# A gated-MLP kernel behind a dynamic convolution: another ramp, moved slots in eight superblocks, and a DMA that transposes for the last two

## The chip, the core and the metric

The kernel runs on one core of a Trainium2 chip. The core has TensorE (PE, matrix multiplies into PSUM), VectorE (DVE), ScalarE (ACT), GpSimd (POOL) and SyncE (SP), each with an instruction queue of its own that runs in order, and 16 DMA engines that work on the transfers which SyncE and GpSimd issue. The metric is the device time of the core in microseconds (us), the median of several executions. The profile is one further execution, recorded by the hardware profiler; its span is shorter than its device time by what lies around the program.

## What is computed

The input x has 8 sequences of 4096 tokens with 192 features. Each token has, for each of 8 heads of 24 features, 7 weights that go through a softmax. The convolution is causal: a token's output is the weighted sum of itself and the six tokens before it, with zeros ahead of a sequence's start. Then comes h = conv @ w_in (192 to 2048), g = h - tanh(h), and out = g @ w_out (2048 to 192).

```
w = exp(weight_gen - max);  w = w / (sum(w) + 1e-09)
x_pad = concatenate([zeros(B, 6, D), x], axis=1)
conv = einsum('bshk,bskhg->bshg', w, x_unf)      # k: 7 taps
h = conv @ w_in;  g = h - tanh(h);  out = g @ w_out
```

Inputs and outputs are float32; inside, the products, the convolution, g and both weight matrices are bfloat16.

## The kernel before

**Tiling.** The 32768 tokens are worked in 32 superblocks n of 1024 tokens. In SBUF a superblock lies with 8 consecutive tokens (j = 0 to 7) on each of 128 partitions. Its x tile (`x_t`, line 130) holds 14 rows of 192: the six tokens before (the halo) and the eight. Two such tiles exist and are used in turn. `load_wg` (L116) and `load_x` (L126) load with SyncE's DMAs.

**The convolution.** For a superblock the softmax is an exp on ScalarE (L169), sums and reciprocals on VectorE (L183, L198), and a scaling (L229) that writes the weights `wsm`. GpSimd multiplies x with the weights tap by tap (`products`, L299): taps 0 to 3 into `pa`, taps 4 to 6 into `pb`. VectorE takes a part of taps 0 and 1 off it (`help`, L250 and L251): it works on x of superblock n+2, and for superblocks 9 to 14 also on x of n+3, at f = 3 and f = 12 of the loop. The seven products are added in two places. DMAs issued by GpSimd that accumulate (`dma_sum`, L236) add `pb` onto `pa` and, from superblock 13 on, two taps of `pa` onto the other two (`second_sum`). What is left (two or four summands) is added by TensorE while it transposes: `conv_sums` (L384) multiplies with an identity and accumulates in PSUM, and ScalarE evicts the transposed convolution into `convT` (L410). There the 192 features lie as 3 slots c of 64 rows, and tokens are in columns; the lower 64 partitions hold even j, the upper 64 odd j, so that both halves of TensorE's rows work at once.

**The two matmuls.** The main loop runs over n and, inside, over 16 tiles f of 128 hidden features. `gemm1` (L427) does six matmuls on 64 rows, alternating between the halves, into one PSUM tile `ph` (three exist). ScalarE takes the tanh (L440), VectorE the difference `gt` (L441). The second matmul (L495) of superblock n-1 is cut into 128 pairs of matmuls on 64 rows, and a hand-written plan says how many pairs stand after each f (`pairs`), at which f and after how many pairs the transposes for superblock n+1 stand (`t1` for the third slot, `t2` for the first two), and at which f the softmax's two half sums stand (`sums`). Superblock 1 has the plan FIRST, 4 to 11 DOUBLE, the others STEADY. Results leave through ScalarE (L514) and SyncE's store (L518); the store of superblock n-2 stands at the start of superblock n.

**The ramp.** Superblocks 0 and 1 are prepared without the loop. There VectorE takes taps too, with weights that it reads from PSUM, and GpSimd reads weights from SBUF. So superblock 0 is scaled twice (once into SBUF, once into PSUM), and superblock 1 once into PSUM with a copy to SBUF by ScalarE (L221). The weight matrix w_in is loaded into the lower 64 partitions (`load_w_in`, L573), with feature 3u + c on partition u in slot c, and copied to the upper 64.

**Order.** Every engine runs its instructions in the order of the program text. A SyncE DMA that has to wait holds those behind it. SyncE's DMAs use eight completion counters in turn, and a DMA that reuses a counter waits until the one before on that counter has landed.

Of the kernel before, what the change touches and what calls it, by code (L numbers as in the profile page):

```python
# [16 lines left out]
def kernel(  # L17
# [28 lines left out]
    TWO_SUMS = (13, 14, 15, 16, 17, 18, 19, 20, 21, 22, 23, 24, 25, 26, 27, 28, 29, 30, 31)  # L46
    AHEAD = 4
# [3 lines left out]
    HELP = {n: ((n - 2, 3),) for n in (4, 5, 6, 7, 8, 9, 10, 11, 12, 13, 14, 15, 16, 17, 18, 19, 20, 21, 22, 23, 24, 25, 26, 27, 28, 29, 30, 31)} | {9: ((7, 3), (6, 12)), 10: ((8, 3), (7, 12)), 11: ((9, 3), (8, 12)), 12: ((10, 3), (9, 12)), 13: ((11, 3), (10, 12)), 14: ((12, 3), (11, 12))}  # L51
# [5 lines left out]
    RELIEF = ()  # L57
    assert S % TOK == 0 and D % R == 0 and F % P == 0
# [3 lines left out]
    xpool = ctx.enter_context(tc.tile_pool(name="xpool", bufs=2))  # L62
# [31 lines left out]
    conv_of = {}  # L94
    g_of = {}
# [19 lines left out]

    def load_wg(n):  # L116
        b, s = divmod(n, NSB)
        s0 = s * TOK
        wg_t = wgpool.tile([P, J, H, K], FP32, name="wg_t")
        nc.sync.dma_start(  # L120
            out=wg_t[:],
            in_=weight_gen[b, s0 : s0 + TOK].rearrange("(p j) h k -> p j h k", p=P),
        )
        wg_of[n] = wg_t

    def load_x(n, behind=None):  # L126
        b, s = divmod(n, NSB)
        s0 = s * TOK

        x_t = xpool.tile([P, HALO + J, D], FP32, name="x_t")  # L130

        def rows(p0, p1, r0=0, r1=HALO + J):
            first = x[0, 0:1]
            return nc.sync.dma_start(  # L134
                out=x_t[p0:p1, r0:r1, :],
                in_=bass.AP(
                    tensor=first.tensor,
                    offset=first.offset + (b * S + s0 + p0 * J - HALO + r0) * D,
                    ap=[[J * D, p1 - p0], [D, r1 - r0], [1, D]],
                ),  # L140
            )

        def no_halo():
            nc.sync.dma_start(  # L144
                out=x_t[0:1, 0:HALO, :],
                in_=zero[:].rearrange("o (h d) -> o h d", h=1).to_broadcast([1, HALO, D]),
            )


        if n == 0:  # L150
            rows(0, P, HALO, HALO + J)
            rows(16, P, 0, HALO)
            rows(1, 16, 0, HALO)
            no_halo()
        else:
            dma = rows(16 if s == 0 and ZERO_AT is None else 0, P)
            if behind is not None:
                order(dma, behind, "order of the loads")
            if s == 0 and ZERO_AT is None:
                rows(0, 16, HALO)  # L160
                rows(1, 16, 0, HALO)
                no_halo()
            elif s == 0:
                halo_of[n] = no_halo
        x_of[n] = x_t
# [40 lines left out]
    def softmax_norm_ramp(n, bank):  # L206
# [9 lines left out]
        wsm_v = bank[:, 0 : J * H * K].rearrange("p (j h k) -> p j h k", j=J, h=H)  # L216
        if n == 0 and SCALE_TWICE:
            scale(nc.vector, wsm[:], e_of[n], zr_v)
# [9 lines left out]
    def scale(eng, wsm, e_t, zr):  # L228
        return eng.tensor_mul(  # L229
            wsm.rearrange("p j h k -> p (j h) k"),  # L230
            e_t[:].rearrange("p j h k -> p (j h) k"),
            zr.rearrange("p (n o) -> p n o", o=1).to_broadcast([P, J * H, K]),
        )
# [9 lines left out]
    def help(n, ph, j):  # L243

        if n not in held:
            held[n] = (x_of[n], wsm_of[n][0], papool.tile([P, KA, J, D], BF16, name="pa"))
        x_t, wsm, pa = held[n]
        x_v = x_t[:]
        w = ph[:, 0, 0 : KH * H].rearrange("p (k h) -> p k h", k=KH)
        nc.vector.tensor_copy(w, wsm[:, j].rearrange("p h k -> p k h")[:, 0:KH])  # L250
        nc.vector.tensor_mul(  # L251
            pa[:, 0:KH, j, :].rearrange("p k (h g) -> p k h g", h=H),
            bass.AP(
                tensor=x_v.tensor,
                offset=x_v.offset + j * D,
                ap=[x_v.ap[0], [D, KH], [G, H], [1, G]],
            ),
            w.rearrange("p k (h o) -> p k h o", o=1).to_broadcast([P, KH, H, G]),
        )

    def products(n, taps=None, sums=None, hooks={}):
# [15 lines left out]
        x_v = x_t[:]  # L277
        step = x_v.ap[0]
# [6 lines left out]
        def mul(eng, k0, k1, j0=0, j1=J):  # L285

            if eng is nc.scalar:
                for j in range(j0, j1):
                    for h in range(H):
                        eng.activation(  # L290
                            out=prod(k0, k1)[:, 0, j, h * G : (h + 1) * G],
                            in_=x_t[:, k0 + j, h * G : (h + 1) * G],
                            func=ACT.Copy,
                            scale=wsm[:, j, h, k0 : k0 + 1],
                        )
                return
            w = wsm_v if eng is nc.vector else wsm[:]
            nj = j1 - j0
            return eng.tensor_mul(  # L299
                prod(k0, k1)[:, :, j0:j1].rearrange("p k j (h g) -> p k (j h) g", h=H),  # L300
                bass.AP(
                    tensor=x_v.tensor,
                    offset=x_v.offset + (k0 + j0) * D,
                    ap=[step, [D, k1 - k0], [G, nj * H], [1, G]],
                ),
                w[:, j0:j1]
                .rearrange("p j h (k o) -> p k (j h) o", o=1)[:, k0:k1]
                .to_broadcast([P, k1 - k0, nj * H, G]),
            )
# [15 lines left out]

        nt = len(HELP.get(n, ()))
        first = mul(nc.gpsimd, 0, KH, 0, J - nt)
        if n in PACED:

            order(first, pace_of[n - 3], "pace")  # L330
        if n in LAST_TAP:

            x_after[n + 1] = mul(nc.gpsimd, KH, KA - 1)
            second_sum(n - 1)
        else:
            mul(nc.gpsimd, KH, KA)
            second_sum(n - 1)
        if n not in LAST_TAP or n not in X_LATE:
            x_after[n + 1] = first

        def rest():
            if n in PART:
                dma_sum(pa[:, 0:2], pa[:, 2:4])
            mul(nc.gpsimd, KA, K)
            if n in PART:
                prods_of[n] = parts(4, 5, 6, 0, 1)
            else:
                dma_sum(pa[:, 0:3], pb[:, 0:3])
                if n in LAST_TAP:
                    mul(nc.gpsimd, KA - 1, KA)  # L350
# [5 lines left out]
                if n == NTOT - 1:  # L356
                    second_sum(n)

        return rest

    def second_sum(n):

        if n in to_sum:
            pa = to_sum.pop(n)
            dma_sum(pa[:, 0:2], pa[:, 2:4])

# [55 lines left out]
    def gemm1(n, f):  # L422
        convT = conv_of[n]
        ph = psum_h.tile([P, 2, HT], FP32, name="ph", tag="ph")
        for c in range(NC):
            for r in range(2):
                nc.tensor.matmul(  # L427
                    ph[:, r, :],
                    lhsT=w_in[r * R : (r + 1) * R, c, f * P : (f + 1) * P],
                    rhs=convT[r * R : (r + 1) * R, c, :],  # L430
                    start=(c == 0),
                    stop=(c == NC - 1),
                )
        th = tpool.tile([P, TOK], FP32, name="th")
# [73 lines left out]
    def store_out(blk):  # L508
# [6 lines left out]
        if j == J - 1:  # L515
# [3 lines left out]
                out=out[n * TOK : (n + 1) * TOK, :].rearrange("(p j) e -> p j e", p=P),  # L519
# [9 lines left out]
    def gemm2_last(j, f0=0, f1=NFT):  # L529
# [20 lines left out]
        ot = tpool.tile([P, D], FP32, name="ot", tag="th")  # L550
        nc.scalar.activation(out=ot[:], in_=po[:, 0, 0:D], func=ACT.Copy)
        nc.vector.tensor_add(out_sb[:, j, :], po[:, 1, 0:D], ot[:])
        if j % 2 == 1:
            nc.sync.dma_start(
                out=out[n * TOK : (n + 1) * TOK, :].rearrange("(p j) e -> p j e", p=P)[
                    :, j - 1 : j + 1, :
                ],
                in_=out_sb[:, j - 1 : j + 1, :],
            )

    w_in = const.tile([P, NC, F], BF16, name="w_in")
    w_out = const.tile([P, NFT, D], BF16, name="w_out")

# [28 lines left out]
    for c in range(NC):  # L592
        load_w_in(c, c + 1, 0, FA, last_exp[0] if c == 0 else None)
# [92 lines left out]
    DOUBLE = dict(pairs=(4, 12, 0, 16, 0, 16, 5, 11, 0, 5, 11, 6, 10, 0, 16, 16), t1=(15, 4), t2=(11, 4), scale=15, sums=(1, 10))  # L686
    DOUBLE_IN = (4, 5, 6, 7, 8, 9, 10, 11)

# [18 lines left out]
    for n in range(1, NTOT):  # L707
        more = n < NTOT - 1
        finish = []
        plan = FIRST if n == 1 else DOUBLE if n in DOUBLE_IN else APART if n in APART_IN else STEADY  # L710

        soft = [m for m in (n + 3 if n <= AHEAD else n + 4,) if m < NTOT]
        for f in range(NFT):
# [13 lines left out]
            elif f == 1:  # L727
                if soft:
                    softmax_exp(soft[0])
                if n + 2 < NTOT:  # L730
# [13 lines left out]
            for m in (n + 2, n + 3):  # L744
                if (n, f) in HELP.get(m, ()):
                    help(m, ph, J - 1 - HELP[m].index((n, f)))
            if n + 2 < NTOT and f == (9 if n == 1 else max([b for a, b in HELP.get(n + 2, ()) if a == n] + [3])):
# [4 lines left out]
            for chunks, at in sorted((((0, 1), plan["t2"]), ((2,), plan["t1"])), key=lambda c: c[1]):  # L752
                if more and at[0] == f:
# [3 lines left out]
                    if chunks == (2,):  # L757
                        finish = [softmax_norm(m, pc[:, 0]) for m in soft]
            if f >= plan["scale"]:
# [45 lines left out]
```

## Time and profile before

| | |
|---|---|
| median of 3 runs | 745.81 us (745.04 to 746.27) |
| the profiled execution: span | 743.4 us |
| TensorE busy | 722.3 us, 97% |
| VectorE busy | 687.4 us, 92% |
| GpSimd busy | 654.5 us, 88% |
| ScalarE busy | 638.8 us, 86% |
| first matmul L427 | 0.379 us mean, 3072 of them |
| second matmul L495 | 0.243 us mean, 7936 of them |
| granted TensorE clock | 0.995 of full speed, mean over the span |

Busy times of TensorE are made of overlapping records, so 97% doesn't say that it is at its peak. What the chain of waits says counts more: from 39 us on it is nearly all TensorE. A superblock takes 21.84 us at the end of the kernel and about 22.65 in superblocks 4 to 11, where the transposes add four summands instead of two. Superblock 31 ends with the second matmul alone, from 729.5 us.

The start of a superblock can be read from SyncE's stores, which stand some 3 us behind it. On the profile's clock superblock 7 begins near 176 us, superblock 8 near 198.7, superblock 30 at 684.3 and superblock 31 at 706.1.

### The profile page before, as it was taken

The page shows a single profiled execution, that of the slowest core. Times are in us where ns is not written, and L with a number is a line of the kernel's source. Part 1 is how long each engine was busy: PE and PEld are TensorE (multiplying, and loading weights), DVE is VectorE, ACT ScalarE, POOL GpSimd, SP SyncE. Part 2 cuts the span into 40 slices and gives each one's busy share as a digit, 9 for nine tenths or more (in the row PEclk, how much of TensorE's full clock was granted, in tenths as well). Part 3 has the DMA queues.
Part 4 walks back from the last instruction along what each step waited for, and adds up shares of the span by engine and source line. Part 5 has one row for each costly group of instructions (what it writes and reads, how often), then busy time and mean ns, then how long its engine had stood idle before and what let it go on. Part 6 is the DMA issues. An engine that isn't in the chain of part 4 may idle for free.

```text
span 743.4 us, 30037 instructions
## 1 busy us (share of the span) xinstructions
PE 722.3 (97%) x13616; PEld 556.5 (75%) x13616; DVE 687.4 (92%) x723; ACT 638.8 (86%) x872; POOL 654.5 (88%) x163
## 2 busy tenths in 40 slices
PE   3899999999999999999999999999999999999997
PEld 2477777778777777777777777777777777877777
DVE  7999899999999999999999999999999999988893
ACT  4888888888888888989889999898998989888882
POOL 7999999999999999999999999999999999991000
PEclk9899999999999999999999999999999999999999
DMA  8925367766567668878777977877887877776112
GB/s 236 245 46 161 135 172 185 195 179 149 124 183 184 183 185 224 210 199 203 166 202 209 236 186 204 178 195 205 221 209 195 192 181 194 193 149 110 45 45 86
DMA packets 34269, 130.06 MB, mean 175 GB/s; under 512 B 4591, under 2 KB 9439, under 8 KB 30174
## 3 DMA queue, kind: packets, MB, share of 16 engines
q0 software_dynamic: 19424, 51.12, 40.4%
q1 hardware_dynamic: 14718, 77.03, 27.6%
q8 instruction: 106, 1.74, 0.9%
q14 instruction: 21, 0.17, 0.1%
HBM read 54.52 MB, written 25.17 MB: 107 GB/s over the span
## 4 chain that ended last, share of the span: by engine, by line
PE 92%; DVE 5%; ACT 1%; issue 1%; DMA 1%; SPq 0%; DVEq 0%
PE ph L427 43%; PE obank L495 43%; PE pc L384 4%; DVE gt L441 3%; PE po L538 1%; ACT th L440 1%; DVE pa L299 1%; DMA wg_t<-in_weight_gen_dram 1%; DVE zsum L183 0%; SPq L134 0%; ACT convT L402 0%; DVE obank L211 0%; DVE pa L251 0%; DVE pb L299 0%; SPq L144 0%
## 5 line engine op out<-in xcount | busy, mean ns | idle before, releaser
L441 DVE TENSOR_TENSOR gt<-ph,th 128x1024 bf16<-128x1024 f32 x512 | 601.6, 1217 | 33.4 <-ACT th L440 23.2
L440 ACT ACTIVATE th<-ph 128x1024 f32<-128x1024 f32 x512 | 512.1, 1025 | 69.2 <-PE ph L427 60.3
L427 PE MATMUL ph<-convT,w_in 64*128 64x512 bf16 x3072 | 415.1, 379 | 5.3 <-DVE gt L441 3.3
L495 PEld LDWEIGHTS <-gt 64*128 64x128 bf16 x7936 | 355.6, 94 | 80.6 <-issue 6.3
L495 PE MATMUL obank<-w_out,gt 64*128 64x192 bf16 x7936 | 408.0, 243 | 0.9 <-issue 0.8
L299 POOL TENSOR_TENSOR pa<-x_t,wsm 128x2688 bf16<-128x2688 f32 (+3 forms) x68 | 338.9, 5232 | 0.2
L299 POOL TENSOR_TENSOR pb<-x_t,wsm 128x4608 bf16<-128x4608 f32 (+2 forms) x33 | 283.8, 8601 | 0.7 <-ACT wsm L221 0.5
L427 PEld LDWEIGHTS <-w_in 64*128 64x128 bf16 x3072 | 163.0, 94 | 86.0 <-issue 18.3
L514 ACT ACTIVATE out_sb<-obank 128x192 f32<-128x192 f32 x248 | 81.3, 328 | 11.2 <-PE obank L495 10.3
L410 ACT ACTIVATE convT<-pc 128x1024 bf16<-128x1024 f32 (+1 forms) x62 | 50.1, 810 | 2.9 <-PE pc L384 2.7
L236 POOL DMA_DIRECT2D pa<-pb x28 | 36.0, 1284 | 13.7 <-POOL pb L299 9.1
L384 PEld LDWEIGHTS <-pa 64*128 64x128 bf16 x2064 | 41.5, 100 | 6.8 <-DVE pa L299 1.1
L236 POOL DMA_DIRECT2D pa<-pa x21 | 34.7, 1651 | 9.6 <-DMA pa<-pb 8.9
L384 PE MATMUL pc<-ident,pa 64*128 64x64 bf16 x1968 | 41.2, 191 | 1.8 <-POOL pa L299 0.9
L183 DVE TENSOR_REDUCE zsum<-wg_t 128x32 f32<-128x224 f32 (+1 forms) x61 | 23.6, 387 | 2.9 <-ACT wg_t L169 2.9
L169 ACT ACTIVATE wg_t<-wg_t 128x448 f32<-128x448 f32 x32 | 18.2, 570 | 6.3 <-DMA wg_t<-in_weight_gen_dram 6.2
L251 DVE TENSOR_TENSOR pa<-x_t,ph 128x384 bf16<-128x384 f32 x34 | 18.8, 554 | 2.0 <-DVE ph L250 0.3
L229 DVE TENSOR_TENSOR wsm<-wg_t,pc 128x448 f32<-128x448 f32 x27 | 16.8, 621 | 2.5
L198 DVE RECIPROCAL pc<-zsum 128x64 f32<-128x64 f32 x27 | 14.9, 550 | 0.0
L384 PE MATMUL pc<-ident,pb 64*128 64x64 bf16 x216 | 4.9, 206 | 9.0 <-POOL pb L299 9.0
L384 PEld LDWEIGHTS <-pb 64*128 64x128 bf16 x288 | 6.3, 106 | 9.5 <-POOL pb L299 9.0
L538 PE MATMUL po<-w_out,gt 64*128 64x192 bf16 x256 | 11.2, 243 | 0.0
(27 smaller groups left out, 56.8 us busy)
## 6 DMA issues: line engine op xcount, KB each, us to landing
x_t<-in_x_dram SPq DMA_DIRECT2D x31, 1344.0 KB, 7.9
pa<-pb POOLq DMA_DIRECT2D x28, 1152.0 KB, 9.5
out_dram<-out_sb SPq DMA_DIRECT2D x31, 768.0 KB, 3.9
pa<-pa POOLq DMA_DIRECT2D x21, 768.0 KB, 7.2
wg_t<-in_weight_gen_dram SPq DMA_DIRECT2D x32, 224.0 KB, 7.1
x_t<-in_x_dram SPq DMA_DIRECT2D x1, 768.0 KB
w_out<-in_moe_w_out_dram POOLq DMA_DIRECT2D x1, 768.0 KB, 9.5
out_dram<-out_sb SPq DMA_DIRECT2D x4, 192.0 KB, 3.0
```

Source lines behind the costliest of these rows:

```text
L183: nc.vector.reduce_sum(out=zsum_of[n][:, j0 * H : j1 * H], in_=e_of[n][:, j0:j1].rearrange("p j h k -> p (j h) k"), axis=AX.X,)
L236: return nc.gpsimd.dma_start(out=out.rearrange("p k j d -> p k (j d)"), in_=in_.rearrange("p k j d -> p k (j d)"), accum_op=mybir.AluOpTyp ...
L251: nc.vector.tensor_mul(pa[:, 0:KH, j, :].rearrange("p k (h g) -> p k h g", h=H), bass.AP(tensor=x_v.tensor, offset=x_v.offset + j * D, ap= ...
L299: return eng.tensor_mul(prod(k0, k1)[:, :, j0:j1].rearrange("p k j (h g) -> p k (j h) g", h=H), bass.AP(tensor=x_v.tensor, offset=x_v.offs ...
L384: nc.tensor.matmul(pc[r][:, col : col + R] if home else pc[:, r, col : col + R], lhsT=prods[c][gi][r * R : (r + 1) * R, 2 * j : 2 * j + 2] ...
L410: last_conv[0] = nc.scalar.activation(out=out, in_=pc[:, :, 0:cols].rearrange("p r (cj t) -> p r cj t", t=R), func=ACT.Copy,)
L427: nc.tensor.matmul(ph[:, r, :], lhsT=w_in[r * R : (r + 1) * R, c, f * P : (f + 1) * P], rhs=convT[r * R : (r + 1) * R, c, :], start=(c == ...
L440: last_act[0] = nc.scalar.activation(out=th[:], in_=ph_f, func=ACT.Tanh)
L441: last_sub[0] = nc.vector.tensor_sub(gt[:], ph_f, th[:])
L495: mm = nc.tensor.matmul(po[:, 0:D], lhsT=g_of[n][f][r * R : (r + 1) * R, col : col + P], rhs=w_out[r * R : (r + 1) * R, f, :], start=(r == ...
L514: last_act[0] = nc.scalar.activation(out=out_sb[:, j, :], in_=po[:, 0:D], func=ACT.Copy)
L538: nc.tensor.matmul(po[:, r, 0:D], lhsT=g_of[n][f][r * R : (r + 1) * R, col : col + P], rhs=w_out[r * R : (r + 1) * R, f, :], start=(f == 0 ...
```

## The change

Everything is in one diff; these are its parts.

- **Ramp.** `RAMP_TAPS`: the scalings of superblocks 0 and 1 are cut by taps, each tap going only to the memory from which it is read; ScalarE's copy for superblock 1 is gone. `W_CUTS`: the first part of w_in comes with one DMA instead of three. Superblocks 0 and 1 share a layout of 16 consecutive tokens on a partition, eight for each (`tokens`), so that superblock 1 finds its halo in superblock 0's rows and loads 8 rows instead of 14. The two x tiles are now two places in one tile `x_ring`, which superblocks 0 and 1 share overlapping; superblock 2 has a tile of its own, whose space is used again for `w_nat`.
- **Deal.** DOUBLE has other numbers: one to three slots of `pairs`, `t1`, `t2` and one of `sums`.
- **Last two superblocks.** For n = 30 and 31 a third accumulating DMA (`third_sum`) leaves the whole convolution in the first tap of `pa`; for 30 it stands in GpSimd's order inside the products of 31, which are cut in two for it. A DMA issued by SyncE (`turn`) transposes it into `convT`. There the 192 features of two tokens lie in three blocks of 128 rows, so `gemm1` does two matmuls on 128 rows and two on 64. TensorE's transposes and ScalarE's evictions for 30 and 31 are gone, and superblocks 29 and 30 have the plan TURNED.
- **w_in in the order of features.** These matmuls need w_in with feature d on partition d. `turn_w_in`, in superblock 7 after f = 3, copies w_in into `w_nat` with twelve DMAs in SyncE's order; each takes every third partition.

```diff
+    THREE = (30, 31)
+    RAMP_TAPS = (((True, 6, 7), (False, 2, 6), (True, 0, 2)), ((True, 4, 7), (False, 0, 2), (True, 2, 4)))
+    W_CUTS = ((0, 3),)
+    NAT_AT = (7, 3)
...
+    x_ring = const.tile([P, 2 * (HALO + J), D], FP32, name="x_ring")
+    def tokens(t, n):
+        if n < 2:
+            return t[0 : 2 * TOK].rearrange("(p s j) ... -> p s j ...", p=P, j=J)[:, n]
+        return t[n * TOK : (n + 1) * TOK].rearrange("(p j) ... -> p j ...", j=J)
...
+        at = {0: 0, 1: J}.get(n, 0 if n % 2 else HALO + J)
+        if n == 2:
+            x_t = npool.tile([P, 2 * J, D], FP32, name="x2", tag="spare")[:, 0 : HALO + J]
+        else:
+            x_t = x_ring[:, at : at + HALO + J]
...
+        if RAMP_TAPS is not None:
+            for to_sbuf, k0, k1 in RAMP_TAPS[n]:
+                ramp_scale[n] = scale(nc.vector, wsm[:] if to_sbuf else wsm_v, e_of[n], zr_v, k0, k1)
+            wsm_of[n] = (wsm, wsm_v, None, None)
+            return
...
+            if n - 1 in whole:
+                mul(nc.gpsimd, KA, K - 1)
+                third_sum(n - 1)
+                mul(nc.gpsimd, K - 1, K)
...
+    def third_sum(n):
+        if n in whole:
+            pa = whole[n]
+            dma_sum(pa[:, 0:1], pa[:, 1:2])
+    def turn(n):
+        pa = whole.pop(n)
+        conv_of[n] = cpool.tile([P, NC, HT], BF16, name="convT")
+        nc.sync.dma_start_transpose(
+            out=conv_of[n][:].rearrange("p c (j t) -> p (c j) t", t=P),
+            in_=pa[:, 0].rearrange("p j d -> p (j d)"),
+        )
...
+        if n in THREE:
+            block = convT[:].rearrange("p c (a t) -> p (c a) t", t=P).rearrange("p (j b) t -> p b j t", b=NC)
+            for r, b, c, p0, p1, last in (
+                (0, 0, 0, 0, P, False),
+                (1, 2, 1, 0, P, False),
+                (0, 1, 2, 0, R, True),
+                (1, 1, 2, R, P, True),
+            ):
+                nc.tensor.matmul(
+                    ph[:, r, :],
+                    lhsT=w_nat_of[0][p0:p1, c, ff],
+                    rhs=block[p0:p1, b],
+                    start=not last,
+                    stop=last,
+                )
...
+    def turn_w_in():
+        w_nat = w_nat_of[0] = npool.tile([P, NC, F], BF16, name="w_nat", tag="spare")
+        for slot, p0, p1, d0 in ((0, 0, P, 0), (1, 0, P, R), (2, 0, R, P), (2, R, P, 0)):
+            for c in range(NC):
+                u = -(-(d0 - c) // NC)
+                first = p0 + NC * u + c - d0
+                rows = -(-(p1 - first) // NC)
+                nc.sync.dma_start(
+                    out=w_nat[first : first + NC * (rows - 1) + 1 : NC, slot, :], in_=w_in[u : u + rows, c, :]
+                )
...
-    DOUBLE = dict(pairs=(4, 12, 0, 16, 0, 16, 5, 11, 0, 5, 11, 6, 10, 0, 16, 16), t1=(15, 4), t2=(11, 4), scale=15, sums=(1, 10))
+    DOUBLE = dict(pairs=(5, 11, 0, 16, 0, 16, 6, 10, 0, 6, 10, 7, 9, 0, 16, 16), t1=(15, 6), t2=(11, 3), scale=15, sums=(1, 11))
+    TURNED = dict(pairs=(5, 11, 0, 16, 3, 13, 6, 10, 0, 6, 10, 5, 11, 5, 11, 16), t1=(16, 0), t2=(16, 0), scale=14, sums=(1, 7))
+    TURN_AT = 13
...
+            if THREE and (n, f) == NAT_AT:
+                turn_w_in()
+            if turned and f == TURN_AT:
+                turn(n + 1)
```

The remaining lines of the diff rewrite `products` and `help` around a shared `tap_product` without another order of work, and bring options that are off (`ACT_OPS`, `BOTH`).

## The prediction

> **What bounds the kernel now.** I read the page's busy shares and chain first, then the groups of the chain's two big lines, then the stretches where the diff acts: the timelines of SyncE, VectorE and GpSimd around superblocks 7 and 8, TensorE's timeline at the end, and the DMA rows.
>
> ```profile
> PE 722.3 (97%) x13616; PEld 556.5 (75%) x13616; DVE 687.4 (92%) x723; ACT 638.8 (86%) x872; POOL 654.5 (88%) x163
> ...
> PE 92%; DVE 5%; ACT 1%; issue 1%; DMA 1%; SPq 0%; DVEq 0%
> ```
>
> TensorE is the chain for 92% of the span; VectorE, at 92% busy, is the next bound. An engine that delays either in its own order moves the end one for one.
>
> ```profile
> 14.42 0.63 DVE L229 TENSOR_TENSOR obank<-wg_t,obank 128x448 f32<-128x448 f32 x1
> 15.08 0.54 ACT L221 ACTIVATE wsm<-obank 128x448 f32<-128x448 f32 x1 [3.03 <-DVE obank L229]
> 15.65 3.42 DVE L299 TENSOR_TENSOR pa<-x_t,obank 128x1536 bf16<-128x1536 f32 x2 [0.61 <-ACT wsm L221]
> ```
>
> The ramp is different: until 39.1 us VectorE is the chain (scalings, then products, then sixteen gt of 1.14 us each), and here it waits 0.61 us for ScalarE's copy.
>
> ```profile
> 182.55 0.33 SPq L134 DMA_DIRECT2D x_t<-in_x_dram  x1
> 182.92 0.92 SPq L120 DMA_DIRECT2D wg_t<-in_weight_gen_dram  x1
> 201.78 0.34 SPq L518 DMA_DIRECT2D out_dram<-out_sb  x1
> 202.30 1.20 SPq L134 DMA_DIRECT2D x_t<-in_x_dram  x1
> ...
> 217.40 0.19 DVE L250 COPY ph<-wsm 128x16 f32<-128x16 f32 x1
> 217.67 0.55 DVE L251 TENSOR_TENSOR pa<-x_t,ph 128x384 bf16<-128x384 f32 x1
> ...
> 217.26 10.33 POOL L299 TENSOR_TENSOR pa<-x_t,wsm 128x2304 bf16<-128x2304 f32 x2
> ```
>
> x of superblock 11 is issued at 202.30 and lands at 213.2 (the trace's last completion). Two readers come at 217.3 and 217.7: GpSimd's first product and the help that stands in VectorE's order in superblock 8. So this load has 4.5 us to spare.
>
> ```profile
> q0 software_dynamic: 19424, 51.12, 40.4%
> q1 hardware_dynamic: 14718, 77.03, 27.6%
> ...
> q1 hardware_dynamic: 602, 1.84, 64.5%
> ...
> DMA packets 13, 0.00 MB, mean 2 GB/s; under 512 B 7, under 2 KB 13, under 8 KB 13
> ```
>
> The third row is SyncE's queue in the first 9.3 us: two wg loads, x in pieces of 128, 112 and 15 rows, and six rows of zeros. One packet per row makes 517; the other 85 are completions, and 85 = 4 x 16 + 15 + 6. So a DMA of 128 or 112 rows ran on 16 DMA engines, one of 15 rows on 15, one of 6 rows on 6: each time a number that divides the rows. The last row, around a lone DMA of zeros, has the same handful.
>
> **The ramp.** (1) Superblock 0: two scalings of 448 become pieces of 64, 256 and 128. Starts are 0.53 us apart for 448, and products of 192 and 1344 (0.35 and 1.55 us) give 1.05 ns an element, so pieces start after 0.13, 0.33 and 0.19: 0.65 us in place of 1.19 (5.19 to 6.38). x lands at 5.91, so VectorE's products begin near 5.95: 0.4 us. GpSimd's first product (5.97) is held by the same landing and gains nothing, nor do fewer issues for w_in ahead of it. (2) Superblock 1: scaling and wait (14.42 to 15.65, 1.23 us) become pieces of 192, 128 and 128: 0.75 us, a gain of 0.5. VectorE is the chain to 39.1, so both count: -0.8 with a little given back (between 0 and -1.0). (3) The shared token layout takes 576 KB off x(1), which lands before its reader either way; x(2) in a tile of its own still stands behind the copy of w_in (19.93) in SyncE's order. Both nothing; if x(1) were late it would be a gain inside the same bounds.
>
> **The new deal.** No instruction is added; pairs of the second matmul, the transposes and one sum move by one or two slots. Stores of out are 23.00, 22.62, 23.27, 22.62, 22.67, 22.67, 22.68 and 22.75 us apart in superblocks 4 to 11. All at the shortest would save 1.3; that is one end, the same loss the other (two more stalls like superblock 6's 0.65). I take -0.5.
>
> **The last two superblocks, removed.**
>
> ```profile
> 701.36 0.65 PE L384 MATMUL pc<-ident,pa 64*128 64x64 bf16 x32
> 701.83 0.84 PE L495 MATMUL obank<-w_out,gt 64*128 64x192 bf16 x16
> ...
> 703.91 0.41 PE L384 MATMUL pc<-ident,pa 64*128 64x64 bf16 x16
> 704.14 0.83 PE L427 MATMUL ph<-convT,w_in 64*128 64x512 bf16 x6
> ```
>
> Start to start the transposes cost 0.47 + 0.23 = 0.70 us of TensorE, twice: -1.4, on the path. ScalarE's evictions (1.02 + 0.60) go too, beside other work.
>
> **The chain put in their place.** For superblock 30 the second sum is issued at 660.13 and lands in 7.5 us. The third waits in GpSimd's queue between two cuts of superblock 31's products, behind it one product and the sum pa<-pb (late by some 1.6 us: two issues and the wait). A sum of 768 KB took 6.4 us and one of 1152 KB 9.9, so 384 KB about 5: landed by 674. SyncE then holds only the transposing DMA, wanted at 684.3. For superblock 31: pa<-pb 672.3 to 682.4, second sum to 689, third to 694, wanted at 706.1 less what is gained. The transposing DMA moves 393 KB as 96 tiles of 16 x 128, which no row shows. One end: like pa<-pa of 768 KB at most, 6.4 us, hidden both times. Other end: in 32-byte pieces at 36 ns, the shortest data packet (768 B), 768 on each engine, 27.6 us: landed at 702, 17 us late for superblock 30. I take the first, to which size and engines are nearest: 0.
>
> **The first matmul of these superblocks.** Six matmuls on 64 rows (0.65 us) become two on 128 rows and two on 64: the same streaming time. But a 128-row matmul needs both halves, which now run staggered. No 128-row matmul is in the trace. Bounds for each of 64 changes of shape (two per f, 32 f): 0, or the whole tail of a matmul, 379 ns less the 215 between starts = 0.164 us, 10.5 in all. The nearest row is a half's offset within a pair of the second matmul (0.082 us a pair, so 0.041): 2.6 us. The Trainium skill, TensorEngine Tiling (Array Packing), section Key Properties, says that changing the tiling mode, unlike changing the tile, drains TensorE; it gives no price. By it the term goes toward the upper bound, 768.6 in all; by the bare streaming row it is 0, 758.1 in all. No row here can show it.
>
> **The copy of w_in.** Twelve DMAs in SyncE's order in superblock 7, between wg at 182.92 and the store at 201.78: four of 43 rows of 4096 B, two of 42, four of 21, two of 22. Each of eight completion counters is reused in turn, and in the program the store and x(11) wait for the last two of 43 rows. 43 is prime: by the pattern of the completions such a DMA runs on one engine, and all four on the same one if they start from the same place. 172 rows are 704 KB; the hardware queue moved 77.03 MB in 27.6% of 16 x 743.4 us, 23.5 KB per us and engine: 30 us, from 189 (x(10) ahead) to 219. Dealt to 16 engines all twelve would be 1.57 MB, 4 us, in a stretch where the queue idles. On the one engine also runs its part of pa<-pb of superblocks 9 and 10 (issued 196.68 and 216.44): 73.7 KB each at 10.6 KB per us, 7 us each if they take turns, little if they overlap. So the last lands between 219 and 232, x(11) some 8 us later, 227 to 240, for readers at 217.7. VectorE stands 9 to 22 us; behind it are the gt of superblock 8, for which TensorE runs out of buffers after about 1.5 us. GpSimd's products 11 start as late, and their transposes move with TensorE. Cost 7 to 21, taken near the middle: +15. If spread, 0.
> The Trainium skill, DMA: Bandwidth & Descriptors, section on why a DMA increments its semaphore by 16, gives that pattern as a rule: the largest number up to 16 that divides the outer size, on the lowest-numbered engines. The 15 and the 6 agree.
>
> **Sum.** -0.8 - 0.5 - 1.4 + 2.6 + 15 = +14.9 on the profiled span of 743.4, so 758.3. The profiled execution lies 2.4 under the median of the runs, 745.81; with that, 760.7.
>
> **Rivals.**
> A, not slower: the four copies of 43 rows are dealt unevenly over the engines (3 rows to most) or x(11) is otherwise in time. For it: the idle DMA stretch from 191.4 to 196.7 takes 4 us. Against: no DMA in the trace ran on a number that doesn't divide its rows. Then -2.7 and the 128-row matmuls decide: 743.1 at no cost there, slower above 2.7 us (0.042 per change).
> B: spread copies, and the full drain of 10.5: 745.8 - 2.7 + 10.5 = 753.6. For it: tails of 0.164 in each matmul record; against: pairs on two halves already overlap.
> C: the transposing DMA in small pieces: 17 us at superblock 30, with spread copies 743.1 + 17 = 760, over the forecast 778. Against: 32-byte packets in no row.
> D: the copies run late but overlap fully with the sums, and nothing is lost at the matmuls: +7 - 2.7, 750.1; part of the forecast's range.
>
> **Numbers.** Forecast with D 0.67, A 0.24, B 0.05, C 0.04. The forecast's own range is 750 to 775. The range reaches down to A: 742.5 to 774. A measurement of this kernel tells apart about 0.2%, 1.5 us. A gives most of faster (0.20), within 0.2% is A with 2 to 4 us of drain (0.04), the rest is slower (0.76).
>
> **What would show it.** In the after-profile: SyncE issuing x(11) near 225 instead of 202, VectorE's help in superblock 8 waiting for that DMA, one store spacing of 32 to 43 us. If that spacing is 22.6, the forecast is wrong and A holds. First gt near 19.9 instead of 20.77; no transposes on TensorE after some 660 us of before's clock; superblocks 30 and 31 no longer per f than 1.32 us (21.84 less 0.70, by 16) if nothing drains; the transposing DMAs landed by 681 and 701 on that clock.

## The result and the profile after

| | before | after |
|---|---|---|
| median | 745.81 us (745.04 to 746.27) | 775.55 us (773.32 to 776.23, 4 runs) |
| span of the profiled execution | 743.4 us | 771.6 us |
| ratio | | 1.0389 (1.0371 to 1.0408) |

The change makes the kernel 3.9% slower. The prediction had the direction and the mechanism, but its sizes were too small: 760.7 with a range up to 774.0, and the median lies 1.55 us above the range. The page of the changed kernel answers to the busy shares and the chain of before; the two rows at the end are TensorE's busy tenths and its granted clock, in 40 slices of the span:

```profile
PE 728.7 (94%) x13456; PEld 549.1 (71%) x13456; DVE 687.9 (89%) x726; ACT 637.2 (83%) x867; POOL 655.7 (85%) x164
...
PE 74%; POOL 12%; DMA 7%; DVE 3%; issue 2%; SPq 2%; ACT 0%; POOLq 0%; DVEq 0%
...
PE   4899999999925999999999999999999999999998
PEclk9999999999976999999999999999999999999999
```

Busy times hardly change, all their shares fall, and the chain, 92% TensorE before, now has DMA and GpSimd in it. Most of the loss has one place: slices 11 and 12 (counted from 0), 212 to 251 us. SyncE's timeline there (start, duration, what is issued):

```profile
184.05 31.93 SPq L626 DMA_DIRECT2D w_nat<-w_in  x12
218.45 0.35 SPq L569 DMA_DIRECT2D out_dram<-out_sb  x1
225.39 0.34 SPq L150 DMA_DIRECT2D x_ring<-in_x_dram  x1
```

The twelve copies hold SyncE's order for 32 us, and x of superblock 11, issued at 202.30 before, goes out at 225.39. Its readers, on VectorE and on GpSimd:

```profile
216.85 0.19 DVE L291 COPY ph<-wsm 128x16 f32<-128x16 f32 x1
239.07 0.56 DVE L263 TENSOR_TENSOR pa<-x_ring,ph 128x384 bf16<-128x384 f32 x1 [22.04 <-DMA x_ring<-in_x_dram]
```

```profile
212.66 8.35 POOL L263 TENSOR_TENSOR pb<-x_ring,wsm 128x4608 bf16<-128x4608 f32 x1 [4.59 <-DMA pa<-pb]
221.30 1.28 POOL L252 DMA_DIRECT2D pa<-pb  x1 [0.30 <-POOL pb L263]
239.10 9.85 POOL L263 TENSOR_TENSOR pa<-x_ring,wsm 128x2304 bf16<-128x2304 f32 x2 [16.51 <-DMA x_ring<-in_x_dram]
```

Both had the data at 217 before; now both stand until 239.1. TensorE's timeline shows what VectorE's stand costs:

```profile
212.64 0.88 PE L418 MATMUL pc<-ident,pa 64*128 64x64 bf16 x48 [0.75 <-DMA pa<-pb]
...
216.37 1.48 PE L546 MATMUL obank<-w_out,gt 64*128 64x192 bf16 x32
239.69 1.46 PE L478 MATMUL ph<-convT,w_in 64*128 64x512 bf16 x6 [21.83 <-DVE pa L263]
240.94 1.17 PE L546 MATMUL obank<-w_out,gt 64*128 64x192 bf16 x12
241.90 1.06 PE L418 MATMUL pc<-ident,pa 64*128 64x64 bf16 x32
242.77 1.13 PE L546 MATMUL obank<-w_out,gt 64*128 64x192 bf16 x20
243.74 0.81 PE L478 MATMUL ph<-convT,w_in 64*128 64x512 bf16 x6
```

The work from 239.69 to 243.74 in the kernel `spread` below, where no load was late:

```profile
216.65 0.82 PE L478 MATMUL ph<-convT,w_in 64*128 64x512 bf16 x6
217.30 0.66 PE L546 MATMUL obank<-w_out,gt 64*128 64x192 bf16 x12
...
219.09 0.81 PE L478 MATMUL ph<-convT,w_in 64*128 64x512 bf16 x6
```

Three things add up. TensorE is idle for 21.83 us. Then the six matmuls of one f take 1.25 us start to start instead of 0.65, and the stretch to 243.74 takes 4.05 us instead of 2.44: 1.6 us. And the transposes at 212.64 wait 0.75 us for a sum that came late. Together 24.2 us. The view by stretches gives the cause of the middle one; its columns are the stretch, its length, the busy time of PE, PEld, DVE, ACT and POOL with instruction counts, the granted clock, and the DMA share with GB/s:

```profile
239.60:243.70 4.10, 4.01 (x70) 3.08 (x72) 3.59 (x5) 1.62 (x2) 4.10 (x2) 0.58 0.00 0
243.70:248.00 4.30, 4.30 (x72) 2.97 (x68) 3.47 (x5) 3.70 (x6) 4.30 (x1) 1.00 0.89 315
```

After the idle time TensorE's granted clock is 0.58 on average over 4.1 us. The Trainium skill, TensorE: Matmul & The Clock Gate, section What's actually happening, has the rule: half rate after an idle window, full rate again after about 3.4 us of work. By that rule the restart would cost an estimated 1.7 us (half of 3.4); the trace agrees with 1.6. In two runs below the restart cost more: 1.97 us in `two43` (granted clock 0.51 over 4.5 us) and 2.66 us in `one_each` (0.50 over 5.6 us), each against the same instructions in `spread`.

Where the 28.2 us of span lie, from the distances of SyncE's stores of out (the two that hold the stall are added):

| stretch | before | after | difference |
|---|---|---|---|
| first store (ramp) | 66.53 | 66.07 | -0.46 |
| superblocks 4, 5, 6 | 68.89 | 67.97 | -0.92 |
| 7 and 8 | 45.29 | 69.55 | +24.26 |
| 9, 10, 11 | 68.10 | 68.42 | +0.32 |
| 29 | 21.87 | 21.58 | -0.29 |
| 30 | 21.81 | 24.32 | +2.51 |
| 31 | 20.76 | 23.25 | +2.49 |

The rest is 0.3 us. The first row is not clear of what varies between executions: in the nine profiled kernels with the new ramp the first store stands at 66.05 to 66.78 us. The second loss is in the last two superblocks; the group of their first matmul, and the start of superblock 30 on TensorE:

```profile
L468 PE MATMUL ph<-convT,w_nat 64*128 64x512 bf16 (+1 forms) x128 | 29.4, 385 | 0.0
```

```profile
707.18 0.92 PE L468 MATMUL ph<-convT,w_nat 128*128 128x512 bf16 x4
707.93 0.58 PE L546 MATMUL obank<-w_out,gt 64*128 64x192 bf16 x10
708.44 0.93 PE L468 MATMUL ph<-convT,w_nat 128*128 128x512 bf16 x4
709.20 1.07 PE L546 MATMUL obank<-w_out,gt 64*128 64x192 bf16 x22
710.20 1.79 PE L468 MATMUL ph<-convT,w_nat 128*128 128x512 bf16 x8
711.83 1.48 PE L546 MATMUL obank<-w_out,gt 64*128 64x192 bf16 x32
```

A lone matmul lasts as long as before (385 against 379 ns) and the group waits for nothing. But from the first matmul to the second matmul's pairs it is 0.75 us where it was 0.65, and ten matmuls of pairs take 0.51 where they took 0.41: 0.1 us at each change between 128 and 64 rows.

The ramp, on VectorE:

```profile
5.40 0.27 DVE L245 TENSOR_TENSOR wsm<-wg_t,obank 128x64 f32<-128x64 f32 x1
5.70 0.43 DVE L245 TENSOR_TENSOR obank<-wg_t,obank 128x256 f32<-128x256 f32 x1
6.17 0.30 DVE L245 TENSOR_TENSOR wsm<-wg_t,obank 128x128 f32<-128x128 f32 x1
6.38 3.54 DVE L263 TENSOR_TENSOR pb<-x_ring,obank 128x1344 bf16<-128x1344 f32 x4
...
15.34 3.41 DVE L263 TENSOR_TENSOR pa<-x_ring,obank 128x1536 bf16<-128x1536 f32 x2
```

Superblock 0's three scalings take 0.98 us from the first to the product (0.30, 0.47 and 0.21 apart), less than the 1.19 of before but more than the 0.65 foretold. They also begin 0.21 us later in this execution (5.40 against 5.19), so the first product starts at 6.38 as before. Superblock 1's second group of products starts at 15.34 instead of 15.65, and the first gt at 20.45 instead of 20.77.

### The profile page after: what moved, and what is told of

The parts are those of the page before. It is cut to its first block, busy times and chain, and to the rows that moved or that the text cites. A ratio compares the mean times of both kernels' runs of the same rounds, so it can differ in the third digit from the quotient of the medians.

```text
span 771.6 us, 29740 instructions
## 1 busy us (share of the span) xinstructions
PE 728.7 (94%) x13456; PEld 549.1 (71%) x13456; DVE 687.9 (89%) x726; ACT 637.2 (83%) x867; POOL 655.7 (85%) x164
## 4 chain that ended last, share of the span: by engine, by line
PE 74%; POOL 12%; DMA 7%; DVE 3%; issue 2%; SPq 2%; ACT 0%; POOLq 0%; DVEq 0%
PE obank L546 34%; PE ph L478 32%; POOL pa L263 6%; POOL pb L263 6%; DMA w_nat<-w_in 4%; PE ph L468 4%; PE pc L418 3%; DMA x_ring<-in_x_dram 2%; DVE gt L492 2%; PE po L589 1%; SPq L626 1%; DVE pa L263 1%; DMA wg_t<-in_weight_gen_dram 1%; ACT th L491 0%; PE obank L418 0%
## 5 line engine op out<-in xcount | busy, mean ns | idle before, releaser
L478 PE MATMUL ph<-convT,w_in 64*128 64x512 bf16 x2880 | 389.4, 379 | 26.4 <-DVE pa L263 21.8
L263 POOL TENSOR_TENSOR pa<-x_ring,wsm 128x2688 bf16<-128x2688 f32 (+3 forms) x66 | 327.2, 5202 | 16.7 <-DMA x_ring<-in_x_dram 16.5
L263 POOL TENSOR_TENSOR pb<-x_ring,wsm 128x4608 bf16<-128x4608 f32 (+2 forms) x33 | 274.3, 8314 | 6.2 <-DMA pa<-pb 5.0
L478 PEld LDWEIGHTS <-w_in 64*128 64x128 bf16 x2880 | 150.9, 94 | 103.5 <-DVE pa L263 22.4
L565 ACT ACTIVATE out_sb<-obank 128x192 f32<-128x192 f32 x248 | 81.2, 327 | 11.1 <-PE obank L546 10.3
L444 ACT ACTIVATE convT<-pc 128x1024 bf16<-128x1024 f32 (+1 forms) x58 | 46.9, 810 | 7.2 <-PE pc L418 7.1
L252 POOL DMA_DIRECT2D pa<-pa x23 | 36.5, 1585 | 15.5 <-DMA pa<-pb 8.7
L263 DVE TENSOR_TENSOR pa<-x_ring,ph 128x384 bf16<-128x384 f32 x34 | 18.8, 554 | 23.9 <-DMA x_ring<-in_x_dram 22.0
L468 PE MATMUL ph<-convT,w_nat 64*128 64x512 bf16 (+1 forms) x128 | 29.4, 385 | 0.0
L468 PEld LDWEIGHTS <-w_nat 64*128 64x128 bf16 (+1 forms) x128 | 6.8, 95 | 18.9 <-issue 18.8
```

What stands on the lines that cost most here:

```text
L252: return nc.gpsimd.dma_start(out=out.rearrange("p k j d -> p k (j d)"), in_=in_.rearrange("p k j d -> p k (j d)"), accum_op=mybir.AluOpTyp ...
L263: return eng.tensor_mul(bass.AP(tensor=out.tensor, offset=out.offset + j0 * D, ap=[out.ap[0], [J * D, nk], [G, run], [1, G]]), bass.AP(ten ...
L444: last_conv[0] = nc.scalar.activation(out=out, in_=pc[:, :, 0:cols].rearrange("p r (cj t) -> p r cj t", t=R), func=ACT.Copy,)
L468: nc.tensor.matmul(ph[:, r, :], lhsT=w_nat_of[0][p0:p1, c, ff], rhs=block[p0:p1, b], start=not last, stop=last,)
L478: nc.tensor.matmul(ph[:, r, :], lhsT=w_in[r * R : (r + 1) * R, c, ff], rhs=convT[r * R : (r + 1) * R, c, :], start=(c == 0), stop=(c == NC ...
L565: last_act[0] = nc.scalar.activation(out=out_sb[:, j, :], in_=po[:, 0:D], func=ACT.Copy)
```

## The experiments

Each median below stands beside runs of the kernel before on the same chip (medians 745.72 and, for `one_each`, 746.15 us), and each ratio is to those. Runs of some kernels with the transposing DMA scatter: `spread` took 749.15 to 758.93 us (two of seven near 758.9), `couples` 747.96 to 757.59, `rows64` 742.98 to 753.79, while `plain`, `ramp_only` and `third_only` stay within 4 us. One profile of each doesn't show why, so the spacings of the stores say more here than small differences of the medians.

### spread: the copies of 43 rows cut into 42 and 1

```diff
-                nc.sync.dma_start(
-                    out=w_nat[first : first + NC * (rows - 1) + 1 : NC, slot, :], in_=w_in[u : u + rows, c, :]
-                )
+                for a, m in ((0, 42), (42, 1)) if rows == 43 else ((0, rows),):
+                    at = first + NC * a
+                    nc.sync.dma_start(
+                        out=w_nat[at : at + NC * (m - 1) + 1 : NC, slot, :], in_=w_in[u + a : u + a + m, c, :]
+                    )
```

> The four copies of 43 rows are cut into 42 rows and 1 row; all else as in the changed kernel. Theory 1 (a copy of 43 rows runs on one DMA engine, and x of superblock 11 waits in SyncE's order and in that engine's queue behind it): the wait of 22.0 us at VectorE's help goes away, x(11) is issued near 202 again, and the time falls by the 24.3 us that superblocks 7 and 8 had grown: 751. Theory 2 (the volume of 1.57 MB, or the issues in SyncE's order, hold it up whatever the rows are): above 770.

Measured: 750.26 us, ratio 1.009 (1.0054 to 1.0126), span 747.4. SyncE's timeline of this kernel:

```profile
183.95 15.06 SPq L628 DMA_DIRECT2D w_nat<-w_in  x16
200.18 0.35 SPq L569 DMA_DIRECT2D out_dram<-out_sb  x1
202.36 0.34 SPq L150 DMA_DIRECT2D x_ring<-in_x_dram  x1
```

The same bytes, moved with four DMAs more, hold SyncE for 15 us instead of 32. x of superblock 11 goes out at 202.36, no engine waits for it, and superblocks 7 to 9 together take 68.1 us as before (68.0). All of the 24 us hangs on how four of the twelve copies divide. (Superblocks 16 to 18 take 67.60 us here against 65.57, with gaps in TensorE's own issue; why is open.) In the completion records a copy of 43 rows ends with one completion, one of 42 rows with fourteen. The Trainium skill, DMA: Bandwidth & Descriptors, section on why a DMA increments its semaphore by 16, states the rule (the largest number up to 16 that divides the outer size: 1 of 43, 14 of 42); it is borne out here. The records don't name the engine; that the four copies of the changed kernel stood in one engine's queue is read from their ends, one after the other (197.85, 206.87, 218.39 and 225.30 us), and from the DMAs between and behind them: the last share of a copy of 42 rows came at 208.32 where its other thirteen were there by 193.93, that of the store at 233.37 (222.68).

### two43: half the dose

As `spread`, but the first two copies of 43 rows stay whole.

```diff
-                for a, m in ((0, 42), (42, 1)) if rows == 43 else ((0, rows),):
+                for a, m in ((0, 42), (42, 1)) if rows == 43 and slot > 0 else ((0, rows),):
```

> Half the dose of the copy: the first two copies of 43 rows are left whole, the other two are cut into 42 rows and 1 as in the kernel with all four cut (span 747.4, median 750.3). Theory, a copy of 43 rows runs on one DMA engine, and the rows queue on it one after the other: 86 rows at the 0.159 us of a 4096-byte packet are 13.7 us, so the engine is done near 207 us, where the second copy of 43 rows landed in the changed kernel (207.1). x of superblock 11 is issued between 202 and 211 and lands by about 217, when its readers come (216.9 to 217.7). A stall of 0 to 3 us, 750.3 to 753: half the dose costs far less than half, because it has to use up the slack of 4.5 us first. Rival, each such copy costs its share wherever it ends (24.3 / 4, about 6 us each, by traffic or by its counter): 12 us of stall, about 762.

Measured: 758.37 us, ratio 1.018 (1.0148 to 1.0212), span 754.7. SyncE's and VectorE's timelines:

```profile
183.57 28.44 SPq L628 DMA_DIRECT2D w_nat<-w_in  x14
212.12 0.38 SPq L569 DMA_DIRECT2D out_dram<-out_sb  x1
212.62 0.35 SPq L150 DMA_DIRECT2D x_ring<-in_x_dram  x1
```

```profile
221.19 0.56 DVE L263 TENSOR_TENSOR pa<-x_ring,ph 128x384 bf16<-128x384 f32 x1 [5.36 <-DMA x_ring<-in_x_dram]
```

Superblocks 7 and 8 take 52.71 us, 7.4 more than before. That is neither the 0 to 3 us of the theory nor the 12 of its rival, and the issue of x says why. It is late by 10.3 us with two such copies (212.62 against 202.36) and by 23.0 with four (225.39): about in proportion to their number, as one serial engine would have it. The stall isn't in proportion: the slack comes off first, x itself landed 8.5 us after its issue here and 13.6 with four, and TensorE's slow restart comes on top. The theory's 207 us for the engine was right (the second copy completed near 206), but it left out that the other copies have rows on this engine too, behind those: their counters came free only up to 212.

### one_each: the four whole copies in four superblocks

```diff
-    NAT_AT = (7, 3)
+    NAT_AT = ((7, 3), (9, 3), (11, 3), (13, 3))
...
+        long = [k for k in copies if k[0] == 43]
+        for rows, slot, c, u, first in [k for k in copies if k[0] != 43 and part == 0] + [long[part]]:
```

> All four copies of 43 rows are left whole, as in the changed kernel, but one stands in each of superblocks 7, 9, 11 and 13 (after f = 3; the eight others all in 7). Theory, the rows queue on one engine, and only what exceeds the slack of 4.5 us before the next x is lost: 86 rows held x back by 10.3 us and 172 rows by 23.0, so 43 hold it back by about 5 us; the stall is 0 to 1.5 us in each of four superblocks, and the whole about the kernel with all copies cut, 750 to 755. Rival, each such copy costs its 6 us wherever it stands (24.3 / 4): 774, as the changed kernel.

Measured: 753.65 us (751.67 to 756.21), ratio 1.0093 (1.0068 to 1.0118). With all four uncut, no engine waited for a load of x in these superblocks; that of superblock 11 went out at 201.86. So the stall comes of such copies in a row (four in the changed kernel, two in `two43`) ahead of a load with 4.5 us to spare; the rival's 774 is out. The median lies in the expected 750 to 755, but not by the expected way, and one copy isn't free either: what stands behind it on its engine is late. SyncE and GpSimd around the second copy:

```profile
230.00 0.62 SPq L632 DMA_DIRECT2D w_nat<-w_in  x1
236.60 0.73 SPq L160 DMA_DIRECT2D x_ring<-zero  x1
```

```profile
213.13 8.34 POOL L263 TENSOR_TENSOR pb<-x_ring,wsm 128x4608 bf16<-128x4608 f32 x1 [5.72 <-DMA pa<-pb]
...
245.02 9.84 POOL L263 TENSOR_TENSOR pa<-x_ring,wsm 128x2304 bf16<-128x2304 f32 x2 [2.21 <-DMA x_ring<-zero]
```

The second line is the six rows of zeros (4.5 KB) ahead of a sequence's start. Five of their shares landed by 238.85, the sixth at 244.85, just after the copy's 244.67, and GpSimd waited 2.21 us for it. The same happened behind the fourth copy (330.76 and 330.94; GpSimd idle for 3.98 us before 331.18, which the profile puts down to a matmul that ended at that time). Behind the first, a sum had its last share 6 us after the others: GpSimd waited 5.72 us (2.1 in `spread`), TensorE 1.9.

The profiled execution is the longest of the four, with a span of 754.3; what the other three lost, no profile shows. GpSimd, 87% busy over the span, was still late at the end. Superblock 30, on GpSimd, SyncE and TensorE:

```profile
675.45 0.91 POOL L252 DMA_DIRECT2D pa<-pa  x1 [0.63 <-DMA pa<-pa]
```

```profile
679.51 1.56 SPq L396 DMA_TRANSPOSE convT<-pa  x1
```

```profile
687.27 1.58 PE L468 MATMUL ph<-convT,w_nat 128*128 128x512 bf16 x4 [3.06 <-DMA convT<-pa]
```

The third sum is issued at 675.45 instead of 667.54 (`spread`), the transposing DMA at 679.51 instead of 672.26, and TensorE waits 3.06 us for it and restarts at a granted clock of 0.50: the spacing of the stores that holds this (29) is 27.15 us instead of 21.69. The chain of DMAs that replaces the transposes is hidden only as long as GpSimd runs ahead.

### rows64: the same chain of DMAs, matmuls on 64 rows only

`spread`, with six matmuls on 64 rows in `gemm1` of superblocks 30 and 31. Their sums there add other features than the reference's; the streaming time is the same.

```diff
-                (0, 0, 0, 0, P, False),
-                (1, 2, 1, 0, P, False),
+                (0, 0, 0, 0, R, False),
+                (1, 0, 0, R, P, False),
+                (0, 2, 1, 0, R, None),
+                (1, 2, 1, R, P, None),
```

> As the run with 42 rows and 1 row, but the first matmul of superblocks 30 and 31 is six matmuls on 64 rows, two halves in turn, as in the other superblocks; it adds up other features there, so those two superblocks' output is not the reference's. Theory (each change between 128 and 64 rows costs some 0.09 us, 64 changes): superblock 30 falls from 24.3 to 21.1 us and superblock 31 from 23.3 to 20.8, 5.7 us less than that run, 743.5 to 745.5. Rival (a transposed convolution that comes late, or w_nat itself): no difference, 751.

Measured: 745.04 us, ratio 1.0016 (0.9987 to 1.0045), span 742.4. Superblock 30 takes 21.00 us instead of 24.31, superblock 31 20.76 instead of 23.25: 5.8 us less, over 64 changes of shape 0.09 us each. The Trainium skill, TensorEngine Tiling (Array Packing), section Key Properties, says that changing the tiling mode drains TensorE; the size is the one that these runs show. Against the kernel before, superblocks 29 and 30 are shorter by 0.22 and 0.81 us (21.65 and 21.00): that is what the transposes of 30 and 31 were worth on TensorE.

### couples: eight changes of shape fewer

```diff
+            four = four[2:] + four[:2] if f in (2, 8) else four
```

> Kernel with all four copies cut (span 747.4, median 750.3); in superblocks 30 and 31, at f = 2 and f = 8, where two f stand back to back, the first does its two matmuls on 64 rows before its two on 128 rows, so that each couple changes shape twice instead of four times. Same matmuls, same sums. Theory, each change of shape costs TensorE about 0.09 us (5.8 us over 64 changes): eight changes fewer are 0.7 us, a couple takes 1.45 instead of 1.63 us, superblock 30 is 23.95 instead of 24.31 and superblock 31 22.89 instead of 23.25; about 749.5. Rival, the cost belongs to a matmul on 128 rows (it waits for both halves of the array whatever came before): a couple stays at 1.63 us, superblocks at 24.31 and 23.25.

Measured: 749.74 us, ratio 1.0076 (1.0043 to 1.011), span 747.6. The median is only 0.5 us from that of `spread`, too little for a measurement of the whole; the spacing tells it. Superblock 30 takes 23.89 us (24.31) and superblock 31 22.82 (23.25), 0.85 us for eight changes, 0.11 each. A couple on TensorE:

```profile
687.22 1.67 PE L470 MATMUL ph<-convT,w_nat 64*128 64x512 bf16 x8
688.73 1.48 PE L548 MATMUL obank<-w_out,gt 64*128 64x192 bf16 x32
```

From its start to the pairs it is 1.51 us, not 1.63. The cost belongs to the change, not to the matmul on 128 rows, since these matmuls are all still there.

### plain, ramp_only and third_only: the other parts alone

`plain` has `THREE = ()`, which leaves the new ramp and the new deal; `ramp_only` has the DOUBLE of before as well. `third_only` is `plain` with the third sum for superblocks 30 and 31, whose one summand TensorE transposes as before: no copy of w_in, no transposing DMA.

```diff
-    THREE = (30, 31)
+    THREE = ()
```

> Ramp and deal alone: no third sum, no transposing DMA, no copy of w_in; the last two superblocks as before. If the gains read from the stores stay (0.5 us at the ramp, 0.9 us in superblocks 2 to 6): 744.5. Rival, that the 0.7 us which superblocks 11 and 12 lost belongs to the deal and not to the late copy: 745.2 or more.

> The new ramp alone: the deal of superblocks 4 to 11 is that of the kernel before, no copy of w_in, no third sum, no transposing DMA. Theory, the ramp gives 0.46 us and the deal some 0.3 to 0.7 more (superblock 6's spacing was 23.27 before, 23.20 with ramp and new deal, 22.53 in three others): first store at 66.3 instead of 66.8, superblocks 4 to 6 at 23.00, 22.62 and 23.27 as before, median 745.2 to 745.5, between the kernel before (745.81) and ramp with deal (744.96). Rival, the deal is worth nothing and the ramp all of the 0.85: 744.9.

> Ramp, deal and the third accumulating DMA, but TensorE transposes the last two superblocks as before, now one summand instead of two; no copy of w_in, no transposing DMA, no matmul on 128 rows. If the third sum is hidden, half of the transposes' 1.4 us goes: 0.7 below the run with ramp and deal alone, 743.8. Rival (the third sum comes late or holds GpSimd up so that TensorE waits): 744.5 or more.

| | median | ratio | span | first store | superblocks 4 to 6 | superblock 30 |
|---|---|---|---|---|---|---|
| plain | 744.96 | 0.9984 (0.9974 to 0.9994) | 743.2 | 66.13 | 68.63 | 21.81 |
| ramp_only | 744.87 | 0.9994 (0.9981 to 1.0006) | 742.5 | 66.38 | 69.09 | 21.81 |
| third_only | 744.96 | 0.9985 (0.9971 to 0.9999) | 742.8 | 66.78 | 67.96 | 21.78 |

The expectation's 66.3 and 66.8 for the first store are 0.25 us above what the traces show (66.07 and 66.53). `plain` is faster than the kernel before by 0.8 us, hardly more than can be measured; `plain` and `ramp_only` both missed their expected medians (744.5, and 745.2 to 745.5). How this is shared between ramp and deal isn't settled: the median of `ramp_only` is as good, its ratio holds 1, and the spacing of superblock 6 differs between kernels with the same deal (23.20 in `plain`, 22.53 or 22.54 in the seven others).

`third_only` missed its expectation of a further gain. The transposes do halve, but the first matmul after them then waits for VectorE:

```profile
700.74 0.41 PE L418 MATMUL pc<-ident,pa 64*128 64x64 bf16 x16
700.98 0.84 PE L546 MATMUL obank<-w_out,gt 64*128 64x192 bf16 x16
701.99 0.82 PE L478 MATMUL ph<-convT,w_in 64*128 64x512 bf16 x6 [0.17 <-DVE gt L492]
```

From 700.74 to 700.98 they now take 0.24 us instead of 0.47; 0.17 of the gain is given back at the next wait for a gt. A reading that fits, and was not tested: the transposes' PSUM tile is one of the three that the first matmul needs.

No kernel with the transposing DMA has a median below that of `plain`.

## Why the prediction was right, and where it was wrong

**What bounds the kernel; the copy's mechanism.** Right. The copies ran on one engine each, the last ended near 225.3 (219 to 232 foretold), x went out at 225.39 (near 225), VectorE's help in superblock 8 waited for it, and the longest spacing of the stores is 40.62 us (32 to 43). `spread` shows it by taking it away, `two43` by the dose.

**The copy's size: the term that failed.** "Cost 7 to 21, taken near the middle: +15" measured +24.26, above its own upper end. The copies ended where they were foretold, in the middle of the bounds; what came behind them was at the top or over it. x took 13.6 us to land, not 8. The 8 is near the median of all such loads in the profile (7.9), but in the kernel before this very load took 10.6 us (202.30 to 212.92 by its completions; the prediction itself reads 213.2). In the changed kernel fifteen of its sixteen completions were there by 235.3, while the sum of `pb` onto `pa` issued at 221.30 was on its way too (that this slowed it was not tested); the last, behind the late shares of the copies (229.2) and of the store (233.4), came at 238.95. VectorE so stood 22.0 us, the top of 9 to 22. TensorE's credit, put at 1.5 us, was 0.2 (22.04 against 21.83): its buffers ran out almost at once. Two terms were not in the sum at all: the restart at a lower clock, 1.6 us, and the transposes' wait for a late sum, 0.75. A stall that idles TensorE costs more than its own length.

**The changes of shape.** "The nearest row is a half's offset within a pair ... 2.6 us" was the wrong row: `rows64` and `couples` give 0.09 to 0.11 us a change, 5.8 us in all, in the middle of the bounds 0 to 10.5. The two prices that the prediction set against each other, bare streaming (758.1) and a full drain (768.6), enclose it.

**The transposes.** -1.4 foretold, -1.0 measured, in `rows64`. In superblock 29 only 0.06 to 0.38 of the 0.70 us came off, by the kernel; in superblock 30 of `rows64` 0.81 did.

**The transposing DMA at 0.** The number held in the changed kernel: the group of L468 waits for nothing. But the reason was too good. From SyncE's issue at 696.30 to the last landing at 707.04 it took 10.7 us, not 6.4, against superblock 30's first matmul at 707.18: 0.1 us was left of the 3 us counted on (landed by 681, wanted at 684.3). In `rows64` TensorE waited 0.32 us for it, in the profile of `one_each` 3.06. The second, at 717.43, landed by 721.2, with ten us to spare. The rival of small pieces falls: its packets are 3072 of 256 bytes for both DMAs.

**The ramp and the deal.** -0.8 foretold, -0.46 at the first store of this one profile, and not clear of what varies between kernels with the same ramp (66.05 to 66.78). Short scalings take longer than a rate by the element says: pieces of 64, 256 and 128 stand 0.30, 0.47 and 0.21 us apart instead of 0.13, 0.33 and 0.19. Superblock 0 gained 0.21 us instead of the 0.54 by elements (and gave it back by a later start), superblock 1 gained 0.3 instead of 0.5 (its pieces take 0.94 us; the prediction wrote 0.75, where its own rate gives 0.65). The deal: -0.5 foretold, -0.6 over superblocks 4 to 6 and 9 to 11 (-0.92 + 0.32), but the experiments don't separate it from what varies between kernels.

**The rivals.** A is what `spread` makes of the kernel, and even so it is not faster: 750.3, since a change of shape costs 0.09 us and A's own bound was 0.042. Faster needed both, spread copies and nearly free changes. The prediction gave it 0.20 of A's 0.24, though with its own 2.6 us for the changes A comes out at -0.1, about even. B and C didn't come. D, the low end, fell with the 24.26.

With the measured sizes the sum reads -0.46 - 0.6 - 1.0 + 5.8 + 24.3 = +28.0, against 28.2 in the spans.

## What to carry to other kernels

Look at the outer size of each DMA before it goes into a queue that something urgent shares: 43 rows ran on one engine and 42 on fourteen, and cutting off one row was worth 24 us here. When a bound is worked out for a late load, take that load's own time to land rather than a median, and the slowest of its shares, on the engine that is busiest; then add the restart of TensorE to the idle time. Work taken off TensorE by a chain of accumulating and transposing DMAs is free only while the engine that issues the chain is ahead, and mixed shapes in its place cost 0.1 us for each change.

## What the runs showed that was not expected

- A change between matmuls on 128 and on 64 rows cost 0.09 us (`rows64`) to 0.11 us (`couples`) of TensorE, and in the profile no single matmul looks longer for it.
- After idle times of 21.8, 5.2 and 3.1 us TensorE came back at about half of its clock (0.58 over 4.1 us in the changed kernel, 0.51 over 4.5 us in `two43`, 0.50 over 5.6 us in `one_each`), so that even a short wait was followed by slow work that cost 1.6 to 2.7 us more.
- A transposing DMA of 393 KB between two SBUF tiles took SyncE 6.5 to 6.6 us to issue in four of the six kernels that were profiled with it and 1.56 in the two others, for the same instruction; the one for superblock 31 took 1.43 to 1.52 each time. From issue to landing it was 10.7 to 11.0 us in the four and 6.6 and 7.7 in the two. What decides this was not tried.
